# Windowed attention with a SoLU layer behind it: the lower words of the 64-bit weights in 32 bits, and their minimum by GpSimd

## Chip, core and metric

One core of a Trainium2 chip runs the whole program. The metric is the device time of one execution in microseconds (us); of several runs the median counts. The engines are named as in the profile: PE (TensorE), DVE (VectorE), ACT (ScalarE), POOL (GpSimd) and SP (SyncE, whose queue issues all the transfers).

## What is computed

Attention in a window of 64 positions for 8 batches of 8 heads (576 positions, 64 columns a head), then for all 4608 tokens a matmul of 512x1024, a SoLU (the value times its softmax), a layer norm and a matmul of 1024x512. The weights come in as 64-bit words, two 32-bit words to a weight, and the core turns them into float32.

```python
def _attn_ref(q, k, v):
    scores = scale * np.matmul(q, k.transpose(0, 1, 3, 2))
    mask = (rel >= 0) & (rel < window)
    scores = np.where(mask, scores, -1000000000.0)
    attn = np.exp(scores - np.max(scores, axis=-1, keepdims=True))
    attn = attn / (np.sum(attn, axis=-1, keepdims=True) + 1e-09)
    return np.matmul(attn, v)

def _moe_ref(x, w_in, w_out, g_ln):
    h = x @ w_in
    e = np.exp(h - np.max(h, axis=-1, keepdims=True))
    solu = h * (e / (np.sum(e, axis=-1, keepdims=True) + 1e-09))
    mu, var = np.mean(solu, axis=-1, keepdims=True), ...
    return ((solu - mu) / np.sqrt(var + 1e-06) * g_ln) @ w_out
```

## The kernel before

The tokens run in 36 tiles of 128. A tile t goes through these steps, each of which stands in the trace under the name of the buffer that it writes: scores on PE (pS), the maximum of a head on DVE (sS and nmx), its exponential on ACT (sS), the scaling by the reciprocal of the sum on POOL (sS), the transposes on PE (pS again), their copies on ACT or DVE (PT), attention times values on PE (pO), the copy for the next matmul (xH), the first matmul (pH), the norm (mst, e), the transposes of e, and the second matmul (pO). The first tiles multiply in plain float32: tiles 0 to 2 in the first matmul (line 575) and tiles 0 and 1 in the second (line 707). All others multiply in three passes, with weights and data split in a rounded high part and the rest (lines 586 and 719). In the early tiles the attention's transposes are done by PE; later ones go by DMA.

The weights come as 8 blocks of 128 x 1024, blocks 0 to 3 of w_in and blocks 4 to 7 of w_out; block 0 is worked on in two halves of 512 columns. A block lands in a raw buffer, of which there are four, so that blocks 4 to 7 must wait for blocks 0 to 3 to be done. It is converted in five steps (function `weight_block`):

- ACT takes the upper words as float32, scales them and drops the sign into the buffer w (line 346);
- ACT turns the lower words into a small integer and writes it as 16 bits into the lower half of the upper word (line 348);
- DVE masks the upper half of the upper word, as 16-bit numbers, so that the sign alone stays (line 351);
- DVE limits w from above (line 353);
- DVE shifts w left by three bits and joins it with that upper word (line 355).

All operations are recorded by a planner first. It puts them in an order for each engine by due times, which it gets from a cost written beside each operation, and by a table of corrections (HINTS). The engines then run in that order: an instruction that waits holds up all that stand behind it on its engine. The due times run back from PE, whose own sequence is nearly as recorded.

Of the kernel before, what the change touches and what calls it, by code (L numbers as in the profile page):

```python
# [9 lines left out]
F32 = mybir.dt.float32  # L10
F32R = mybir.dt.float32r
BF16 = mybir.dt.bfloat16
U16 = mybir.dt.uint16
U32 = mybir.dt.uint32
I32 = mybir.dt.int32
AF = mybir.ActivationFunctionType
ALU = mybir.AluOpType
# [3 lines left out]
WIN = 64  # L21
BIG = 3.0e38

EXP_LO = 2.0 ** -15
EXP_HI = 122879.9921875
EXP_SCALE = 2.0 ** -112
NEG = -8.0e9
# [6 lines left out]
COLD = 23000  # L34

HINTS = {
    ("ACT", "PT", 0, 0): 1000, ("ACT", "mst", 0, 0): 3750, ("ACT", "raw", "w", 0): 3350,
# [3 lines left out]
    ("ACT", "raw", "w", 5): -65650, ("ACT", "w", 0, 5): -5850, ("DVE", "PT", 0, 5): 11750,  # L41
    ("ACT", "H", 0, 6): 1200, ("ACT", "w", 0, 6): -2400, ("DVE", "mst", 0, 6): 700, ("DVE", "sS", 0, 7): -400,
# [4 lines left out]
}  # L47
BEHIND = 2

EARLY = 3  # L50

PLAIN_IN = 3
SHARED = (0, 1, 2, 3, 4, 5, 6, 7)
PLAIN_OUT = 2

CROSS_FROM = 3
# [165 lines left out]
def tile_window_attention_solu_moe(  # L222
# [17 lines left out]
    nc = tc.nc  # L240
# [5 lines left out]
    H = 2 * NPAIR  # L246
    D = P // 2
# [27 lines left out]
    for first in (0, None, 1):  # L275
        t = masks[first] = const.tile([P, P], F32, name=f"mask{first}")
# [11 lines left out]
    plan = Plan(RINGS, NTILE, NW)  # L288

    def T(tag, n, shape, dtype=F32, pool=None):  # L290

        if (tag, n) not in plan.tiles:
            plan.tiles[tag, n] = (pool or sb).tile(
                shape, dtype, tag=tag, name=f"{tag}_{n}", bufs=RINGS[tag])
        return plan.tiles[tag, n]
# [8 lines left out]
    def W32(i):  # L304
        return T("w", i, [P, 2, 512])
# [9 lines left out]
    def weight_block(i, src):  # L315

        def raw():
            return T("raw", i, [P, 2, 512, 2], I32)  # L320

        def t():
            return W32(i).bitcast(I32)

        def tf():
            return W32(i)

        def lo():
            return raw()[:, :, :, 0]

        def hi():
            return raw()[:, :, :, 1]

        def half(k):
            return raw().bitcast(U16).rearrange("p a n (w k) -> p a n w k", k=2)[:, :, :, 1, k]


        parts = (0, 1) if i == 0 else (slice(0, 2),)
        for x in parts:
            n = 1024 if i else 512  # L340
            R, W = ("raw", i, x), ("w", i) if i else ("w", i, x)
            plan.dma(P * 8 * n, lambda x=x: nc.sync.dma_start(
                raw()[:, x].rearrange("p a n w -> p a (n w)" if i else "p n w -> p (n w)"), src[:, x]), [], [R])
            if i in SHARED:
                A, B = R + ("sign",), R + ("low",)
                plan.op("ACT", n + 66, lambda x=x: nc.scalar.activation(  # L346
                    tf()[:, x], hi()[:, x].bitcast(F32), AF.Abs, scale=EXP_SCALE), [R], [W])
                plan.op("ACT", n + 66, lambda x=x: nc.scalar.activation(  # L348
                    half(0)[:, x], lo()[:, x].bitcast(U32), AF.Copy, bias=-0.47, scale=255 / 256 * 2.0 ** -29),
                    [R, W], [B])  # L350
                plan.op("DVE", n // 3 * 2 + (18 if i else 78), lambda x=x: nc.vector.tensor_scalar(
                    half(1)[:, x], half(1)[:, x], 0x8000, 0, ALU.bitwise_and, ALU.bitwise_or), [R, W], [A], port=True)
                plan.op("DVE", n // 3 * 2 + (18 if i else 78), lambda x=x: nc.vector.tensor_scalar_min(
                    tf()[:, x], tf()[:, x], EXP_HI * EXP_SCALE), [W], [W], port=True)
                plan.op("DVE", n + 170, lambda x=x: nc.vector.scalar_tensor_tensor(
                    t()[:, x], t()[:, x], 3, hi()[:, x], ALU.logical_shift_left, ALU.bitwise_or),
                    [R, A, B], [W], port=True)
                continue
            plan.op("ACT", n + 66, lambda x=x: nc.scalar.activation(
                tf()[:, x], hi()[:, x].bitcast(F32), AF.Abs), [R], [W])  # L360
            plan.op("DVE", n // 3 * 2 + (18 if i else 78), lambda x=x: nc.vector.tensor_scalar(
                tf()[:, x], tf()[:, x], EXP_LO, EXP_HI, ALU.max, ALU.min), [W], [W], port=True)
            plan.op("DVE", n // 3 * 2 + (18 if i else 78), lambda x=x: nc.vector.tensor_scalar(
                t()[:, x], t()[:, x], 0x07FFFFFF, 3, ALU.bitwise_and, ALU.logical_shift_left), [W], [W], port=True)
            plan.op("DVE", n + 170, lambda x=x: nc.vector.scalar_tensor_tensor(
                t()[:, x], hi()[:, x], -0x40000000, t()[:, x], ALU.bitwise_and, ALU.bitwise_or), [R, W], [W], port=True)
            plan.op("DVE", n + 170, lambda x=x: nc.vector.scalar_tensor_tensor(
                t()[:, x], lo()[:, x], 29, t()[:, x], ALU.logical_shift_right, ALU.bitwise_or), [R, W], [W], port=True)

    def prep(i):  # L370
        if i < NC:
            weight_block(i, w_in[i * P:(i + 1) * P, :].rearrange("p (a n) -> p a n", a=2))
        else:
            f = 2 * (i - NC)
            weight_block(i, w_out[f * P:(f + 2) * P, :].rearrange("(a p) n -> p a n", p=P))
# [498 lines left out]
```

## Time and profile before

| what | value |
|---|---|
| runs | 528.54, 526.91, 528.2 us; median 528.2 |
| profiled execution | 526.66 us, its span 524.9 us |
| granted clock of PE | 0.999 |
| busy in the span | PE 505.3 us, DVE 403.0, ACT 372.4, POOL 301.4 |
| chain that ended last | PE 90%, ACT 8%, DMA 1% |
| HBM read and written | 50.86 MB and 9.44 MB |

The span runs from the first to the last instruction of the profiled execution; 1.76 us of that execution's time lie around it. A busy time says how long an engine worked, not whether anything waited for it. The chain of waits is followed back from the last instruction, at each step to what released it; the table of waits says which instruction of an engine stood still, and for whom; the windows cut the span in stretches and say how busy each engine was in each.

### The profile page before, as it was taken

Reading aid. Unit: us, or ns where it says so; the run is one execution under the profiler, and the core shown is the slowest. Engines: PE = TensorE matmul, PEld = TensorE weight load, DVE = VectorE, ACT = ScalarE, POOL = GpSimd, SP = SyncE. Lnnn points to the kernel's source line nnn. Section 1 sums busy time; section 2 is a strip of 40 time slices with the busy share of each in tenths; the row PEclk is TensorE's granted clock in tenths of the full one; section 3 lists DMA queues with packets and bytes.
Section 4 is the critical chain, followed back from the end, with each engine's and each line's share of the span. In section 5 each row is a group of like instructions: output and inputs, shape, how many; then the busy total and the mean of one; then the engine's idle time right before and its main releaser. Section 6 shows DMA issues by size and latency. Waiting matters only on the chain.

```text
span 524.9 us, 11600 instructions
## 1 busy us (share of the span) xinstructions
PE 505.3 (96%) x4072; PEld 394.2 (75%) x4072; DVE 403.0 (77%) x1174; ACT 372.4 (71%) x968; POOL 301.4 (57%) x550
## 2 busy tenths in 40 slices
PE   2798999999999999999999999999999999999996
PEld 2445576788787878888888888888888878888775
DVE  4887988979796978787878787878788688877631
ACT  5999996868686767676686868676858486766331
POOL 2038287584858485848384848584848384746420
PEclk9999999999999999999999999999999999999999
DMA  8994226976788888787999796969796979554301
GB/s 328 404 402 149 92 47 137 250 161 147 158 227 160 205 168 223 157 220 154 226 149 235 131 251 131 253 136 246 145 239 126 217 156 216 114 128 104 77 21 41
DMA packets 148507, 93.57 MB, mean 178 GB/s; under 512 B 132960, under 2 KB 132960, under 8 KB 148064
## 3 DMA queue, kind: packets, MB, share of 16 engines
q1 hardware_dynamic: 148448, 92.83, 72.9%
q8 instruction: 32, 0.52, 0.4%
q14 instruction: 27, 0.22, 0.1%
HBM read 50.86 MB, written 9.44 MB: 115 GB/s over the span
## 4 chain that ended last, share of the span: by engine, by line
PE 90%; ACT 8%; DMA 1%; DVE 0%; issue 0%; SPq 0%; ACTq 0%
PE pO L719 36%; PE pH L586 35%; PE pO L543 7%; PE pS L446 6%; ACT raw L348 3%; PE pO L707 3%; ACT sS L466 2%; ACT w L346 1%; PE pH L575 1%; DMA raw<-w_in 1%; PE pS L683 1%; ACT PT L524 1%; ACT e L603 0%; PE pS L519 0%; ACT xH L553 0%; DVE yL L694 0%
## 5 line engine op out<-in xcount | busy, mean ns | idle before, releaser
L484 POOL TENSOR_SCALAR sS<-sS,rec 128x128 f32<-128x128 f32 x280 | 151.8, 561 | 50.1 <-DVE rec L482 40.8
L466 ACT ACTIVATE sS<-sS,nmx 128x128 f32<-128x128 f32 x288 | 111.4, 389 | 2.1 <-DVE nmx L461 2.1
L719 PE MATMUL pO<-w_outH,yH 128*128 128x512 f32 x272 | 110.2, 405 | 0.0
L719 PE MATMUL pO<-w,yH 128*128 128x512 f32 x272 | 108.0, 397 | 0.0
L719 PE MATMUL pO<-w_outH,yL 128*128 128x512 f32 x272 | 106.8, 393 | 0.0
L586 PE MATMUL pH<-w_inH,xH 128*128 128x512 f32 x264 | 105.9, 401 | 0.0
L586 PE MATMUL pH<-w,xH 128*128 128x512 f32 x264 | 104.2, 398 | 0.0
L586 PE MATMUL pH<-w_inH,xL 128*128 128x512 f32 x264 | 103.6, 392 | 0.0
L498 ACT COPY raw<-sS 128x1024 uint16<-128x1024 uint16 x62 | 64.9, 1047 | 28.3 <-POOL sS L484 28.3
L623 POOL TENSOR_SCALAR e<-e,mst 128x512 f32<-128x512 f32 x72 | 72.9, 1021 | 3.9
L508 DVE COPY PT<-raw 128x1024 uint16<-128x1024 uint16 x62 | 50.1, 808 | 32.4 <-DMA raw<-raw 32.3
L557 ACT CAST xH<-pO 128x512 fp32r<-128x512 f32 x33 | 19.3, 584 | 62.2 <-PE pO L543 62.2
L719 PEld LDWEIGHTS pO<-w_outH,yH 128*128 128x128 f32 x272 | 51.0, 187 | 14.9 <-issue 2.4
L719 PEld LDWEIGHTS pO<-w_outH,yL 128*128 128x128 f32 x272 | 51.1, 188 | 12.8
L601 DVE TENSOR_REDUCE mst<-pH 128x1 f32<-128x1024 f32 x36 | 44.0, 1221 | 21.4 <-PE pH L586 21.1
L586 PEld LDWEIGHTS pH<-w_inH,xH 128*128 128x128 f32 x264 | 49.5, 187 | 13.6 <-DVE mst L606 0.2
L719 PEld LDWEIGHTS pO<-w,yH 128*128 128x128 f32 x272 | 51.1, 188 | 10.9
L609 POOL TENSOR_SCALAR mst<-mst 128x1 f32<-128x1 f32 x36 | 18.1, 501 | 71.5 <-DVE mst L606 65.4
L586 PEld LDWEIGHTS pH<-w_inH,xL 128*128 128x128 f32 x264 | 49.6, 188 | 12.6 <-DVE xL L558 0.2
L586 PEld LDWEIGHTS pH<-w,xH 128*128 128x128 f32 x264 | 49.6, 188 | 11.5 <-issue 0.2
L612 ACT ACTIVATE sq<-e,mst 128x1024 bf16<-128x1024 f32 x36 | 41.4, 1150 | 20.5 <-POOL mst L609 20.5
L615 POOL TENSOR_SCALAR mst<-mst 128x1 f32<-128x1 f32 x36 | 13.7, 380 | 73.3 <-DVE mst L611 38.5
(66 smaller groups left out, 856.6 us busy)
## 6 DMA issues: line engine op xcount, KB each, us to landing
qk<-qk SPq DMA_DIRECT2D x36, 640.0 KB, 5.5
v<-vS SPq DMA_DIRECT2D x36, 512.0 KB, 5.5
y<-ot SPq DMA_DIRECT2D x36, 256.0 KB, 2.5
raw<-w_out SPq DMA_DIRECT2D x4, 1024.0 KB, 9.6
raw<-w_in SPq DMA_DIRECT2D x3, 1024.0 KB, 11.0
raw<-raw SPq DMA_TRANSPOSE x124, 3.2
raw<-w_in SPq DMA_DIRECT2D x2, 512.0 KB, 5.8
g_sb<-gT SPq DMA_DIRECT2D x1, 4.0 KB, 13.3
```

Source lines behind the costliest of these rows:

```text
L446: nc.tensor.matmul(PS(t)[half * WIN:(half + 1) * WIN, r, p], q[rs, p, half * WIN:(half + 1) * WIN], keys, start=True, stop=True)
L466: plan.op("ACT", 390, lambda h=h: nc.scalar.activation(SS(t)[:, h], SS(t)[:, h], AF.Exp, bias=cols("nmx", h), scale=-1.0, accum_out=cols(" ...
L484: plan.op(engine, cost, lambda h=h: v.tensor_scalar(SS(t)[:, h], SS(t)[:, h], rec()[:, h:h + 1], 0.0, ALU.mult, ALU.add), [R], [("sS", t, ...
L498: plan.op("ACT", 1050, lambda x=x: nc.scalar.copy(XP(t)[:, x], SS(t)[:, 4 * x:4 * x + 4].bitcast(U16).rearrange("p h (n w) -> p w (h n)", ...
L508: plan.op("DVE", 740, lambda x=x: nc.vector.tensor_copy(PT(t)[:, 4 * x:4 * x + 4].bitcast(U16).rearrange("p h (n w) -> p h w n", w=2), XP( ...
L543: nc.tensor.matmul(PX(t)[r * D:(r + 1) * D, p, ks], V(t, half)[:, h * D:(h + 1) * D], PT(t)[:, h, ks], start=True, stop=True)
L557: plan.op("ACT", 560, lambda: nc.scalar.copy(XH(t), PX(t)), [("pO", NTILE + t)], [("xH", t)])
L586: plan.op("PE", 235, lambda n=n, c=c, x=x, w=w: nc.tensor.matmul(PH(t)[:, hs], x(t)[:, c], WH(c, h) if w is WH else WL(c)[:, h], start=(n ...
L601: plan.op("DVE", 1225, lambda: nc.vector.tensor_reduce(nmax(), PH(t), axis=AX.X, op=ALU.max, negate=True), [("pH", t)], [key(0)])
L612: plan.op("ACT", 1150, lambda: nc.scalar.activation(T("sq", t, [P, DFF], BF16), E(t), AF.Square, bias=nmean(), scale=1.0, accum_out=ss()), ...
L623: plan.op("POOL", 770, lambda h=h, hs=hs: nc.gpsimd.tensor_scalar(E(t)[:, hs], E(t)[:, hs], nmean(), kk(), ALU.add, ALU.mult), [key(4), ke ...
L719: plan.op("PE", 235, lambda f=f, i=i, x=x, k=k, y=y, w=w: nc.tensor.matmul(PO(), y(t)[:, f], w(i, x), start=(f == k == 0), stop=(f == NF - ...
```

## The change

The lower words stay where they are. ACT converts them in place and writes them as 32-bit words (line 352 of the changed kernel) in place of the 16-bit write into the upper word. DVE's mask of the sign goes. Two DVE instructions of the shift-and-join kind take the place of one: the first joins the sign of the upper word with the converted lower word, the second shifts w and joins it with that (lines 376 and 379). The minimum goes from DVE to POOL, in halves of 512 columns (line 363). With these go new costs for the planner and a new table of corrections, which set the order on all engines; the sequence of the first 20 transfers on SP stays as it was, and PE's sequence changes in the first three tiles only.

```diff
 HINTS = {
...
-    ("ACT", "raw", "w", 5): -65650, ("ACT", "w", 0, 5): -5850, ("DVE", "PT", 0, 5): 11750,
...
+    ("DVE", "rec", 0, 4): -4300, ("DVE", "y", 0, 4): 82050, ("ACT", "raw", "w", 5): -119200,
...
-SHARED = (0, 1, 2, 3, 4, 5, 6, 7)
+HELPED = (0, 1, 2, 3, 4, 5, 6, 7)
+MASKED = 0
...
-            if i in SHARED:
-                A, B = R + ("sign",), R + ("low",)
-                plan.op("ACT", n + 66, lambda x=x: nc.scalar.activation(
-                    tf()[:, x], hi()[:, x].bitcast(F32), AF.Abs, scale=EXP_SCALE), [R], [W])
-                plan.op("ACT", n + 66, lambda x=x: nc.scalar.activation(
-                    half(0)[:, x], lo()[:, x].bitcast(U32), AF.Copy, bias=-0.47, scale=255 / 256 * 2.0 ** -29),
-                    [R, W], [B])
-                plan.op("DVE", n // 3 * 2 + (18 if i else 78), lambda x=x: nc.vector.tensor_scalar(
-                    half(1)[:, x], half(1)[:, x], 0x8000, 0, ALU.bitwise_and, ALU.bitwise_or), [R, W], [A], port=True)
-                plan.op("DVE", n // 3 * 2 + (18 if i else 78), lambda x=x: nc.vector.tensor_scalar_min(
-                    tf()[:, x], tf()[:, x], EXP_HI * EXP_SCALE), [W], [W], port=True)
-                plan.op("DVE", n + 170, lambda x=x: nc.vector.scalar_tensor_tensor(
-                    t()[:, x], t()[:, x], 3, hi()[:, x], ALU.logical_shift_left, ALU.bitwise_or),
-                    [R, A, B], [W], port=True)
-                continue
...
+            ab = 1139 if i else 644
+            plan.op("ACT", ab, lambda x=x: nc.scalar.activation(
+                tf()[:, x], hi()[:, x].bitcast(F32), AF.Abs, scale=EXP_SCALE), [R], [W])
+            if not MASKED:
+                plan.op("ACT", ab + (206 if i else 69), lambda x=x: nc.scalar.activation(
+                    lo()[:, x], lo()[:, x].bitcast(U32), AF.Copy, bias=-0.47, scale=255 / 256 * 2.0 ** -29), [R], [B])
+            halves = [x] if i == 0 else [0, 1]
...
+            if helped:
+                for y in halves:
+                    plan.op("POOL", 720, lambda y=y: nc.gpsimd.tensor_scalar_min(
+                        tf()[:, y], tf()[:, y], EXP_HI * EXP_SCALE), [W], [W + (y,)])
...
+                plan.op("DVE", n + 200, lambda x=x: nc.vector.scalar_tensor_tensor(
+                    lo()[:, x], hi()[:, x], -0x80000000, lo()[:, x], ALU.bitwise_and, ALU.bitwise_or),
+                    [R], [B], port=True)
+                plan.op("DVE", n + 200, lambda x=x: nc.vector.scalar_tensor_tensor(
+                    t()[:, x], t()[:, x], 3, lo()[:, x], ALU.logical_shift_left, ALU.bitwise_or),
+                    [R, B], [W, *C], port=True)
```

ACT, from the conversion of block 3 to the copies of the transposes of tile 1, before. Block 3 is raw_155 and w_265, block 4 is raw_250 and w_295; sS_247 and PT_343 belong to tile 1, sS_314 to tile 2.

```order
L346 ACTIVATE w_265<-raw_155 128x1024
L348 ACTIVATE raw_155<-raw_155 128x1024
L466 ACTIVATE sS_247,sm_253<-sS_247,nmx_248 128x128 x7
L346 ACTIVATE w_295<-raw_250 128x1024
L348 ACTIVATE raw_250<-raw_250 128x1024
L466 ACTIVATE sS_314,sm_321<-sS_314,nmx_315 128x128 x2
L524 COPY PT_343<-pS_324 128x512
L466 ACTIVATE sS_314,sm_321<-sS_314,nmx_315 128x128
L603 ACTIVATE e_360,mst_332<-pH_212,mst_332 128x1024
L553 COPY xH_377<-pO_350 128x256
L524 COPY PT_343<-pS_324 128x512
```

The same place in the changed kernel: block 3 is raw_154 and w_258, block 4 is raw_262 and w_303, block 5 is raw_267; sS_235 and PT_344 belong to tile 1, sS_321 to tile 2.

```order
L349 ACTIVATE w_258<-raw_154 128x1024
L352 ACTIVATE raw_154<-raw_154 128x1024
L479 ACTIVATE sS_235,sm_252<-sS_235,nmx_236 128x128 x7
L352 ACTIVATE raw_262<-raw_262 128x1024
L349 ACTIVATE w_303<-raw_262 128x1024
L352 ACTIVATE raw_267<-raw_267 128x1024
L537 COPY PT_344<-pS_327 128x512
L479 ACTIVATE sS_321,sm_346<-sS_321,nmx_322 128x128
L616 ACTIVATE e_362,mst_333<-pH_254,mst_333 128x1024
L566 COPY xH_381<-pO_349 128x256
L537 COPY PT_344<-pS_327 128x512
```

The lower words of block 5 now stand ahead of the first copy of tile 1's transposes, and two exponentials of tile 2 went behind it. Further up in the queue the same instructions stand in both, in an order that differs a little.

POOL, from its first instruction on a tile or a weight, before: sS_247, sS_314 and sS_399 are the scores of tiles 1, 2 and 3, the mst are small columns of the norm.

```order
L484 TENSOR_SCALAR sS_247<-sS_247,rec_289 128x128 x8
L609 TENSOR_SCALAR mst_332<-mst_332 128x1
L484 TENSOR_SCALAR sS_314<-sS_314,rec_429 128x128 x8
L484 TENSOR_SCALAR sS_399<-sS_399,rec_461 128x128 x8
L609 TENSOR_SCALAR mst_464<-mst_464 128x1
```

The same place in the changed kernel, where sS_235, sS_321 and sS_406 are the scores of tiles 1, 2 and 3, w_137, w_180, w_220 and w_258 are blocks 0 to 3, and w_303 and w_429 are blocks 4 and 5:

```order
L363 TENSOR_SCALAR w_137<-w_137 128x512 x2
L363 TENSOR_SCALAR w_180<-w_180 128x512 x2
L363 TENSOR_SCALAR w_220<-w_220 128x512 x2
L363 TENSOR_SCALAR w_258<-w_258 128x512 x2
L497 TENSOR_SCALAR sS_235<-sS_235,rec_291 128x128 x6
L363 TENSOR_SCALAR w_303<-w_303 128x512 x2
L497 TENSOR_SCALAR sS_235<-sS_235,rec_291 128x128 x2
L622 TENSOR_SCALAR mst_333<-mst_333 128x1
L363 TENSOR_SCALAR w_429<-w_429 128x512
L497 TENSOR_SCALAR sS_321<-sS_321,rec_434 128x128 x8
L363 TENSOR_SCALAR w_429<-w_429 128x512
L497 TENSOR_SCALAR sS_406<-sS_406,rec_460 128x128 x4
```

The minimum of block 4 now stands between the scaled heads of tile 1, and the two halves of block 5 stand ahead of tile 2 and of tile 3.

More of the change, by code (lines that the diff above doesn't have):

```diff
@@ L22 @@
 BIG = 3.0e38
-EXP_LO = 2.0 ** -15
 EXP_HI = 122879.9921875
@@ L36 @@
 HINTS = {
-    ("ACT", "PT", 0, 0): 1000, ("ACT", "mst", 0, 0): 3750, ("ACT", "raw", "w", 0): 3350,
[3 rows of a table removed]
-    ("ACT", "raw", "w", 5): -65650, ("ACT", "w", 0, 5): -5850, ("DVE", "PT", 0, 5): 11750,
-    ("ACT", "H", 0, 6): 1200, ("ACT", "w", 0, 6): -2400, ("DVE", "mst", 0, 6): 700, ("DVE", "sS", 0, 7): -400,
[4 rows of a table removed]
+    ("ACT", "mst", 0, 0): 3700, ("ACT", "raw", "w", 0): 34400, ("ACT", "xH", 0, 0): 3450,
+    ("DVE", "w", 0, 0): 1100, ("ACT", "mst", 0, 1): 6800, ("ACT", "w", 0, 1): -1800,
+    ("POOL", "sS", 0, 1): 26650, ("ACT", "mst", 0, 2): -22350, ("ACT", "xH", 0, 2): 800,
+    ("PE", "pS", 0, 2): -3200, ("ACT", "raw", "w", 3): 1150, ("ACT", "yH", 0, 3): 87000,
+    ("DVE", "PT", 0, 3): -3700, ("DVE", "raw", "w", 3): 11950, ("DVE", "xL", 0, 3): -14900,
+    ("DVE", "y", 0, 3): 10000, ("POOL", "sS", 0, 3): -950, ("ACT", "xH", 0, 4): -300,
+    ("ACT", "yH", 0, 4): -10100, ("DVE", "e", 0, 4): 6450, ("DVE", "mst", 0, 4): 24250,
+    ("DVE", "rec", 0, 4): -4300, ("DVE", "y", 0, 4): 82050, ("ACT", "raw", "w", 5): -119200,
+    ("ACT", "w", 0, 5): -8750, ("DVE", "e", 0, 5): 14000, ("ACT", "ot", 0, 6): 24300, ("ACT", "w", 0, 6): -4550,
+    ("DVE", "rec", 0, 6): -18500, ("DVE", "w", 0, 11): 17650, ("DVE", "w", 0, 13): 1300,
+    ("ACT", "sS", 0, 32): 52450, ("POOL", "sS", 0, 32): 28350, ("DVE", "mst", 0, 33): -10700,
[4 rows of a table added]
 }
@@ L332, in hi @@
             return raw()[:, :, :, 1]
-        def half(k):
-            return raw().bitcast(U16).rearrange("p a n (w k) -> p a n w k", k=2)[:, :, :, 1, k]
         parts = (0, 1) if i == 0 else (slice(0, 2),)
@@ L343, in weight_block @@
                 raw()[:, x].rearrange("p a n w -> p a (n w)" if i else "p n w -> p (n w)"), src[:, x]), [], [R])
-            if i in SHARED:
-                A, B = R + ("sign",), R + ("low",)
-                plan.op("ACT", n + 66, lambda x=x: nc.scalar.activation(
-                    tf()[:, x], hi()[:, x].bitcast(F32), AF.Abs, scale=EXP_SCALE), [R], [W])
-                plan.op("ACT", n + 66, lambda x=x: nc.scalar.activation(
-                    half(0)[:, x], lo()[:, x].bitcast(U32), AF.Copy, bias=-0.47, scale=255 / 256 * 2.0 ** -29),
-                    [R, W], [B])
-                plan.op("DVE", n // 3 * 2 + (18 if i else 78), lambda x=x: nc.vector.tensor_scalar(
-                    half(1)[:, x], half(1)[:, x], 0x8000, 0, ALU.bitwise_and, ALU.bitwise_or), [R, W], [A], port=True)
+            B = R + ("low",)
@@ new lines, in weight_block @@
+            S = R + ("sign",)
+            ab = 1139 if i else 644
[5 more added lines that the diff above has]
+            halves = [x] if i == 0 else [0, 1]
@@ new lines, in weight_block @@
+            helped = i in HELPED
+            C = [W + (y,) for y in halves] if helped else []
+            D = [S + (y,) for y in halves] if MASKED else []
+            for y in halves if MASKED else []:
+                plan.op("POOL", 770, lambda y=y: nc.gpsimd.tensor_scalar(
+                    hi()[:, y], hi()[:, y], -0x80000000, 0, ALU.bitwise_and, ALU.bitwise_or), [R, W], [S + (y,)])
+            if helped:
+                for y in halves:
+                    plan.op("POOL", 720, lambda y=y: nc.gpsimd.tensor_scalar_min(
+                        tf()[:, y], tf()[:, y], EXP_HI * EXP_SCALE), [W], [W + (y,)])
+            else:
@@ L353, in weight_block @@
                 plan.op("DVE", n // 3 * 2 + (18 if i else 78), lambda x=x: nc.vector.tensor_scalar_min(
                     tf()[:, x], tf()[:, x], EXP_HI * EXP_SCALE), [W], [W], port=True)
-                plan.op("DVE", n + 170, lambda x=x: nc.vector.scalar_tensor_tensor(
+            if MASKED:
+                plan.op("DVE", n + 200, lambda x=x: nc.vector.scalar_tensor_tensor(
                     t()[:, x], t()[:, x], 3, hi()[:, x], ALU.logical_shift_left, ALU.bitwise_or),
-                    [R, A, B], [W], port=True)
@@ L358, in weight_block @@
-                continue
[L359 to L368, printed above, removed]
+                    [R, *D], [W, *C], port=True)
+                plan.op("DVE", n + 200, lambda x=x: nc.vector.scalar_tensor_tensor(
+                    t()[:, x], lo()[:, x], 29, t()[:, x], ALU.logical_shift_right, ALU.bitwise_or),
+                    [R], [W], port=True)
+            else:
+                plan.op("DVE", n + 200, lambda x=x: nc.vector.scalar_tensor_tensor(
+                    lo()[:, x], hi()[:, x], -0x80000000, lo()[:, x], ALU.bitwise_and, ALU.bitwise_or),
+                    [R], [B], port=True)
+                plan.op("DVE", n + 200, lambda x=x: nc.vector.scalar_tensor_tensor(
+                    t()[:, x], t()[:, x], 3, lo()[:, x], ALU.logical_shift_left, ALU.bitwise_or),
+                    [R, B], [W, *C], port=True)
```

11 rows, old and new, of the table HINTS are left out of this document.

## The prediction

> **What bounds the kernel now.** I read the page's busy times first, then the windows, the table of PE's waits, and the chain of waits in the stretch where they lie.
>
> ```profile
> PE 505.3 (96%) x4072; PEld 394.2 (75%) x4072; DVE 403.0 (77%) x1174; ACT 372.4 (71%) x968; POOL 301.4 (57%) x550
> ```
>
> PE is busy for 505.3 of a span of 524.9 us. The windows show where the other 19.6 us lie; the columns are the stretch, its length, then the busy time (and count) of PE, weight loads, DVE, ACT and POOL, the granted clock, and the share and rate of the DMA engines.
>
> ```profile
> 20.00:30.00 10.00, 8.80 (x52) 4.21 (x44) 6.86 (x23) 9.24 (x22) 0.20 (x1) 1.00 1.02 402
> 30.00:40.00 10.00, 9.02 (x106) 5.26 (x99) 9.43 (x43) 9.94 (x26) 4.01 (x9) 1.00 1.01 396
> 40.00:50.00 10.00, 8.46 (x87) 5.10 (x87) 8.21 (x25) 9.78 (x27) 8.75 (x17) 1.00 0.38 122
> ...
> 100.00:500.00 400.00, 400.00 (x3279) 324.43 (x3279) 317.61 (x912) 279.24 (x752) 253.55 (x444) 1.00 0.79 175
> 500.00:524.90 24.90, 20.54 (x95) 15.87 (x93) 5.37 (x9) 6.55 (x11) 3.04 (x7) 0.98 0.09 33
> ```
>
> From 100 to 500 us PE is busy for 400.00 of 400 us: nothing that other engines do faster there can shorten it. At the end it idles for 4.4 us, but PE's sequence and the few operations of the last norm stand there as before. What the change can win lies in the first 60 us, where ACT is busy for 9.2 to 9.9 of every 10 us and the DMA engines are full until 40 us. PE's waits say the same, all of them before 50 us:
>
> ```profile
> PE pO L543 <- ACT PT L524: 2.9, 2, 1.7
> PE pH L575 <- ACT xH L553: 1.6, 1, 1.6
> PE pS L519 <- ACT PT L524: 1.0, 1, 1.0
> PE pS L519 <- POOL sS L484: 0.9, 2, 0.5
> ```
>
> So the front of the program is ACT's queue, and a microsecond that it wins there reaches the end as long as no other wait takes its place. The chain of waits (start, length, what) shows that queue:
>
> ```profile
> 7.21 1.54 ACT sS L466 x8
> ...
> 33.27 0.48 ACT PT L524
> 33.75 0.39 ACT sS L466 x2
> 34.14 1.09 ACT e L603 x2
> 35.24 0.32 ACT xH L553
> 35.56 0.49 ACT PT L524
> ...
> 38.23 1.06 ACT w L346
> ```
>
> An exponential with its accumulator read takes 1.54 / 4 = 0.385 us, and a conversion of upper words (line 346) 1.06 us from start to start.
>
> **The change, part by part.** The instructions of the conversion (shortest, median and longest in ns; of nine, seven are of 1024 columns and two of 512):
>
> ```profile
> L346 ACT ACTIVATE w<-raw x9: 644/1144/1227, 6.5 to 52.4; 128x1024 f32<-128x1024 f32 x7, 128x512 f32<-128x512 f32 x2
> L351 DVE TENSOR_SCALAR raw<-raw x9: 734/1311/1411, 7.5 to 54.8; 128x1024 uint16<-128x1024 uint16 x7, 128x512 uint16<-128x512 uint16 x2
> L348 ACT ACTIVATE raw<-raw x9: 1324/2514/2528, 10.8 to 54.0; 128x1024 uint16<-128x1024 uint32 x7, 128x512 uint16<-128x512 uint32 x2
> L355 DVE SCALAR_TENSOR_TENSOR w<-w,raw x9: 693/1225/1601, 12.1 to 56.7; 128x1024 int32<-128x1024 int32 x7, 128x512 int32<-128x512 int32 x2
> ...
> L353 DVE TENSOR_SCALAR w<-w x9: 420/726/894, 11.5 to 55.9; 128x1024 f32<-128x1024 f32 x7, 128x512 f32<-128x512 f32 x2
> ```
>
> DVE loses nine masks (2 x 0.73 + 7 x 1.31 = 10.6 us) and nine minima (2 x 0.42 + 7 x 0.73 = 5.9 us) and gets nine more joins (2 x 0.69 + 7 x 1.23 = 10.0 us): 6.5 us less. I cost that at nothing, since the chain in the front runs on ACT; if DVE did come to bound, the first join of a block is the place, as it now waits for ACT's lower words and holds DVE's queue.
>
> ACT's lower words cost 2 x 1.32 + 7 x 2.51 = 20.2 us now. No row shows the new form, an ACTIVATE that reads and writes 32-bit words at every second place. The nearest row is line 346, of the same engine, count and 32-bit type, with the same stride on the reading side, at 1.144 us. The other end is line 348's own 2.514 us, since the slow part may be the integer input and not the 16-bit output. I take 1.144 (1.06 from start to start) and keep 2.51 as a rival.
>
> The Trainium skill's page "ScalarE: Activation LUTs", section "What ACT_TABLE_LOAD costs", gives an ACTIVATE with immediate scale and bias 186 ns plus 0.833 ns an element, for every function, fp32 and bf16 alike; the estimate from that for 1024 columns is 1.04 us. Line 346 agrees within a tenth, while line 348 stands at 2.51 us, so a type or a place can cost what the rule doesn't have. By the rule the sum below would stay where it is, as a transfer ends last there.
>
> POOL gets 16 minima of 128x512. Its nearest row is line 623, of that shape; two windows (POOL's column is the fifth) show eight scalings of 128x128 with and without DVE at work in the same memory.
>
> ```profile
> L623 POOL TENSOR_SCALAR e<-e,mst x72: 757/1106/1692, 51.8 to 509.4; 128x512 f32<-128x512 f32 x72
> 40.00:45.20 5.20, 0.00 (x0) 5.10 (x8) 1.00 0.25 99
> 46.30:49.20 2.90, 0.00 (x0) 2.80 (x8) 1.00 0.73 226
> ```
>
> A minimum costs 0.76 us when undisturbed and at most 1.69; sixteen are 12 to 27 us, on an engine that is busy for 13 of the 30 us from 20 to 50. Eight scalings take 2.8 us while DVE reads PSUM and 5.1 us beside DVE's masks, minima and joins.
>
> **How the path moves.** The place to count is the first copy of tile 1's transposes on ACT (33.3 us in the chain). Ahead of it stand, before and now, the same conversions of upper words and the same copies; the lower words of blocks 0 to 4 become those of blocks 0 to 5, and 18 exponentials become 16. Without waits ACT would be there at 33.3 - 5 x 2.51 + 6 x 1.06 - 2 x 0.385 = 26.3 us, 7.0 us earlier. But two of these blocks have to land first:
>
> ```profile
> 17.38 0.39 SPq L342 DMA_DIRECT2D raw<-w_out  x1
> raw<-w_out SPq DMA_DIRECT2D x1, 1024.0 KB, 8.8
> 21.81 0.38 SPq L342 DMA_DIRECT2D raw<-w_out  x1
> raw<-w_out SPq DMA_DIRECT2D x1, 1024.0 KB, 6.9
> ```
>
> Block 4 lands at 17.38 + 8.8 = 26.2 us and block 5 at 21.81 + 6.9 = 28.7 us, in a stretch where the DMA engines are full (share 1.02 and 1.01) and the sequence of transfers is as before. An earlier issue moves these landings little; I take them as they are. After 26.2 us ACT still has block 4's lower and upper words and, from 28.7 us, block 5's lower words: the copy starts at 28.7 + 1.06 = 29.8 us. **Of the 7.0 us that ACT saves there, 3.5 are left; the rest becomes a wait for transfers.** If block 5 landed two microseconds sooner, block 4 would bound at 26.2 + 3 x 1.06 = 29.4 us, so this matters little.
>
> From that copy the next five operations of ACT are the same in both orders (copy, exponential, e, xH, copy), 0.48 + 0.39 + 1.09 + 0.32 + 0.49 us, so the first matmul of tile 1 moves by the same 3.5 us, if POOL keeps up. POOL scales six heads of tile 1, then waits for block 4's upper words (28.3 us), does its two minima (29.8) and scales the last two heads (30.5); they are needed at 29.8 + 0.5 + 0.4 + 1.1 + 0.3 = 32.1 us. That leaves 1.6 us.
>
> ```profile
> 36.72 7.13 PE L575 MATMUL pH<-w,xH 128*128 128x512 f32 x16
> 49.21 1.88 PE L575 MATMUL pH<-w,xH 128*128 128x512 f32 x4
> 51.37 5.32 PE L575 MATMUL pH<-w,xH 128*128 128x512 f32 x12
> 59.71 7.13 PE L707 MATMUL pO<-w,yH 128*128 128x512 f32 x16
> ```
>
> Tile 1's first matmul then runs from 33.2 to 40.3 us. Between it and tile 2's stands POOL. On ACT seven exponentials and xH follow the second copy, so block 5's upper words end at 32.1 + 0.5 + 2.7 + 0.3 + 1.1 = 36.7 us; the first half of its minimum ends at 37.5, tile 2's heads at 40.3 (2.8 us) or 42.6 (5.1), the other half at 41.1 or 43.4, tile 3's heads with a small column between at 44.3 or 48.9. ACT, with eight exponentials, two operations of 1.1 us, a copy and e in between, reaches tile 2's second copy at about 44 us. PE's transposes of tile 3 take 0.5 us, so tile 2's first matmul starts between 45 and 49.4 us and, at 7.1 us, ends between 52 and 56.5; now it ends at 56.6. That is a gain of 4.5 at best and nearly nothing at worst. I take the quick row for most of it, because in that stretch DVE's queue holds maxima and sums from PSUM and waits for the exponentials, with one pair of joins: 3.5 us.
>
> Behind it PE has no wait now, in the same sequence as before. The second matmul of tile 0 (59.71, then 56.2) needs block 7: its upper words on ACT by about 49 us, POOL's four minima of blocks 6 and 7 behind the two halves of e by 51 (54 at the slow price), a join of 1.23 us. That is done before 56.2 in both cases. The other queues keep their sequence from there but for a few rows, such as a store that SP now issues ahead of two loads; with 400.00 of 400 us busy on PE and DVE at 318 I cost those at nothing, as DVE's free fifth hides them.
>
> The sum against the profiled execution's own 526.66 us: 526.66 - 3.5 = 523.2 us. The median of the runs shown, 528.2, stands 1.5 us higher, so the forecast there is **524.7 us**. A difference of 0.3% (1.6 us) is about what a measurement of this kernel can tell from none.
>
> **The rivals.** First, that POOL takes the place of ACT. The heads of tiles 2 and 3 stand behind block 5's minima, and beside DVE's two joins each block a scaling costs 0.64 in place of 0.35 us. Then tile 2's first matmul starts at 48.5 to 49.4 us, and 0.1 to 1 us is left: 526.66 - 0.6 = 526.1, at the median 527.6 us. For it speaks the slow window above; against it that in the new order DVE mostly waits there. I give it 0.16. The Trainium skill states a rule on this, on the page "SBUF — State Buffer", section "SBUF: two separate sides": GpSimd and VectorE share a port pair that is locked for a whole instruction by a GpSimd operation or by a VectorE operation with two inputs in that memory, and the loser waits it out. The two windows agree with that rule, and by it the move of the minimum to GpSimd beside more joins is wrong.
>
> Second, on the slower side, that the lower words get no cheaper, because the integer input and not the 16-bit output is what costs 2.51 us. Then ACT has six of them ahead of tile 1's copy and not five, and two exponentials fewer: 2.51 - 0.77 = 1.7 us later at the point that sets the front, and no transfer hides it. The time would be 526.66 + 1.7 = 528.4, at the median 529.9 us. It decides from 6 x = 5 x 2.51 + 0.77, that is x = 2.2 us an instruction. For it speaks that no row has a 32-bit integer input without the slow price; against it that 16-bit output at every fourth place is just as much unlike all the quick rows. This is also the case in which the change doesn't do what it says. I give it 0.12.
>
> **How the numbers follow.** The forecast has 0.72. Its own range goes from a gain of 4.7 us at the profiled execution's level (522.0) to one of 1.8 us at the median's (526.4). The first rival at 527.6 is taken in, so the range ends at 528.2; the second, with 0.12, is left out above. Faster by over 0.3% is the forecast alone, 0.72; within 0.3% the first rival, 0.16; slower the second, 0.12.
>
> **What would show it.** The lower words' row should read 1.1 to 1.4 us; 2.2 or more makes the forecast wrong. ACT's queue should show a new wait, for a transfer from w_out, of some 2 us before block 4. Tile 1's first matmul should start near 33.2, tile 2's end near 53, tile 0's second start near 56.2 us, and from 100 to 500 us PE should be busy throughout. Scalings of tiles 2 and 3 at 0.6 us each, with PE waiting for POOL, would be the first rival.

## The result and the profile after

The changed kernel takes 533.04 us (median of 533.47, 533.36, 532.71 and 531.99), the kernel before, on the same chip, 528.04 us: a ratio of 1.0099 with a 95% interval of 1.0081 to 1.0118. It is slower by 1%; the forecast was 0.7% faster. The profiled execution of the changed kernel has a span of 531.7 us, 6.8 us more than before's 524.9, and a granted clock of 0.988 in place of 0.999. (The medians differ by 5.0 us; what follows accounts for the 6.8 of the two profiled executions.)

The page after, busy times and the chain that ended last, by engine and by line:

```profile
PE 507.5 (95%) x4072; PEld 395.9 (74%) x4072; DVE 400.7 (75%) x1165; ACT 364.0 (68%) x968; POOL 331.7 (62%) x566
...
PE 87%; POOL 6%; DMA 2%; DVE 2%; ACT 1%; issue 1%; SPq 0%; ACTq 0%; DVEq 0%
PE pO L732 36%; PE pH L599 35%; PE pO L556 6%; PE pS L459 6%; PE pO L720 3%; POOL w L363 3%; POOL sS L497 2%; DMA raw<-w_in 2%; PE pS L696 1%; POOL e L636 1%; DVE w L379 1%; DVE raw L376 1%; ACT w L349 0%; PE pS L532 0%; DVE sS L474 0%
```

ACT had 8% of the chain before and has 1% now; POOL had none to speak of and has 6%. The two new instructions, by their lines (shortest, median and longest in ns):

```profile
L363 POOL TENSOR_SCALAR w<-w x16: 1483/1517/2567, 7.1 to 61.5; 128x512 f32<-128x512 f32 x16
...
L352 ACT ACTIVATE raw<-raw x9: 639/1155/1200, 11.2 to 53.8; 128x1024 int32<-128x1024 uint32 x7, 128x512 int32<-128x512 uint32 x2
```

The lower words fell from 2.51 to 1.155 us. The minimum costs POOL 1.52 us for 512 columns, twice the 0.76 us of the row that the prediction took, and never less than 1.48. PE's waits after, below the 5.0 us for the first transfer (total, times, longest, in us):

```profile
PE pS L532 <- ACT PT L537: 3.9, 1, 3.9
PE pS L532 <- DVE sS L497: 3.1, 1, 3.1
PE pS L532 <- POOL sS L497: 2.6, 1, 2.6
PE pO L720 <- DVE yH L701: 2.5, 1, 2.5
```

The first two of these rows end by 15.3 us, in tile 0; before, PE waited 3.3 us for the same heads on DVE and 1.7 us for a copy there. The last two are new, and both hang on POOL, as the chain of waits after shows (start, length, what; pieces under 0.1 us are left out):

```profile
13.85 3.57 POOL w L363 x2
...
26.02 1.23 DVE w L379
...
27.67 3.20 POOL sS L497 x6
30.87 2.91 POOL w L363 x2
33.78 1.45 POOL sS L497
35.28 0.83 PE pS L532 x2
36.11 1.92 PE pS L459 x32
38.02 1.07 PE pO L556 x16
...
41.03 1.04 ACT w L349
42.15 1.50 POOL w L363
43.65 2.81 POOL sS L497 x8
46.46 1.45 POOL w L363
47.92 2.47 POOL sS L497 x4
...
53.41 3.57 POOL e L636 x2
57.07 5.97 POOL w L363 x4
63.10 1.11 issue
64.21 0.69 DVE yH L701
64.94 8.83 PE pO L720 x16
```

From 42 to 63 us POOL is the chain almost without a gap. The four minima of blocks 6 and 7 end at 63.04. DVE's queue at that place (in brackets the idle time and what ended it):

```profile
60.07 1.62 DVE L379 SCALAR_TENSOR_TENSOR w<-w,raw 128x1024 int32<-128x1024 int32 x1 [3.71 <-POOL w L363]
...
63.06 1.23 DVE L379 SCALAR_TENSOR_TENSOR w<-w,raw 128x1024 int32<-128x1024 int32 x1 [0.36 <-POOL w L363]
64.21 1.28 DVE L701 TENSOR_TENSOR yH<-pS,g_sb 128x512 f32<-128x512 f32 x2
```

The second joins of blocks 6 and 7 wait there for the minima, and yH, for which PE waits, stands behind them. The three float32 matmuls after, on PE:

```profile
39.00 8.37 PE L588 MATMUL pH<-w,xH 128*128 128x512 f32 x16
52.38 7.03 PE L588 MATMUL pH<-w,xH 128*128 128x512 f32 x16
64.94 8.83 PE L720 MATMUL pO<-w,yH 128*128 128x512 f32 x16 [2.54 <-DVE yH L701]
```

Tile 1's first matmul starts 2.3 us later than before (39.00 against 36.72), tile 0's second 5.2 us later (64.94 against 59.71). Two of the three also take longer, 8.37 and 8.83 us where the same sixteen matmuls took 7.13. The windows tell why (the granted clock is the number behind POOL's count):

```profile
35.00:40.00 5.00, 4.72 (x51) 3.38 (x52) 3.08 (x21) 2.62 (x11) 0.82 (x3) 0.50 0.82 296
60.00:65.00 5.00, 2.46 (x68) 1.98 (x66) 4.57 (x5) 2.63 (x13) 4.30 (x4) 1.00 0.44 146
65.00:70.00 5.00, 5.00 (x8) 2.16 (x9) 4.93 (x10) 3.35 (x8) 0.21 (x1) 0.66 0.22 90
100.00:500.00 400.00, 400.00 (x3293) 324.50 (x3286) 322.79 (x944) 281.73 (x763) 254.05 (x442) 1.00 0.80 179
```

Behind PE's waits of 2.58 us (up to 35.28) and 2.54 us (up to 64.94) the clock is granted at 0.50 and 0.66 in these windows. Tile 0's second matmul starts 5.2 us late and takes 1.70 us longer: 6.9 us in all, the 6.8 us of the span. The 1.24 us of tile 1's first matmul don't come on top: the chain doesn't run through it, but from PE's scores (36.11) and attention (38.02) over ACT to POOL's minimum at 42.15. Those short steps of PE ran at 0.50 too: the transposes, scores and attention from 35.28 on took 0.83, 1.99 and 1.12 us, where the same steps take 0.44 (at 32.26), 1.10 (at 61.30) and 0.69 us (at 50.84) with the clock at 1.00. An estimate from these figures gives the clock 0.4 + 0.9 + 0.4 + 1.7 = 3.4 us and the waits proper the other 3.5; that nothing else would have held up ACT and POOL in between is not shown. (In the first 20 us the clock's column says less than it seems to: it reads 1.00 there, yet the same 32 scores take 1.98 us at 5.03 and 1.99 us at 17.42.) From 100 to 500 us PE is busy throughout, as before.

### The profile page after: what moved, and what is told of

It is laid out like the page before. It is cut to its first block, busy times and chain, and to the rows that moved or that the text cites. A ratio compares the mean times of both kernels' runs of the same rounds, so it can differ in the third digit from the quotient of the medians.

```text
span 531.7 us, 11605 instructions
## 1 busy us (share of the span) xinstructions
PE 507.5 (95%) x4072; PEld 395.9 (74%) x4072; DVE 400.7 (75%) x1165; ACT 364.0 (68%) x968; POOL 331.7 (62%) x566
## 4 chain that ended last, share of the span: by engine, by line
PE 87%; POOL 6%; DMA 2%; DVE 2%; ACT 1%; issue 1%; SPq 0%; ACTq 0%; DVEq 0%
PE pO L732 36%; PE pH L599 35%; PE pO L556 6%; PE pS L459 6%; PE pO L720 3%; POOL w L363 3%; POOL sS L497 2%; DMA raw<-w_in 2%; PE pS L696 1%; POOL e L636 1%; DVE w L379 1%; DVE raw L376 1%; ACT w L349 0%; PE pS L532 0%; DVE sS L474 0%
## 5 line engine op out<-in xcount | busy, mean ns | idle before, releaser
L636 POOL TENSOR_SCALAR e<-e,mst 128x512 f32<-128x512 f32 x72 | 74.1, 1038 | 3.8
L599 PEld LDWEIGHTS pH<-w_inH,xH 128*128 128x128 f32 x264 | 49.5, 187 | 13.5 <-ACT sS L479 0.2
L479 ACT ACTIVATION_READ_ACCUMULATOR sS<-sS,nmx 128x1 f32 x288 | 54.2, 188 | 0.0
```

Of the source, the lines that this page charges most:

```text
L479: plan.op("ACT", 390, lambda h=h: nc.scalar.activation(SS(t)[:, h], SS(t)[:, h], AF.Exp, bias=cols("nmx", h), scale=-1.0, accum_out=cols(" ...
L599: plan.op("PE", 235, lambda n=n, c=c, x=x, w=w: nc.tensor.matmul(PH(t)[:, hs], x(t)[:, c], WH(c, h) if w is WH else WL(c)[:, h], start=(n ...
L636: plan.op("POOL", 770, lambda h=h, hs=hs: nc.gpsimd.tensor_scalar(E(t)[:, hs], E(t)[:, hs], nmean(), kk(), ALU.add, ALU.mult), [key(4), ke ...
```

## The experiments

All times below are medians; ratios are to runs of the kernel before on the same chip, with 95% intervals.

| kernel | time, us | ratio |
|---|---|---|
| e1, minimum with two operations | 523.69 | 0.9934 (0.9909 to 0.9959) |
| e12, the same again | 523.20 | 0.9922 (0.9909 to 0.9934) |
| e2, multiplication and addition | 523.15 | 0.9917 (0.9903 to 0.9932) |
| e7, one multiplication | 532.79 | 1.0102 (1.0086 to 1.0119) |
| e9, quick minimum twice | 532.55 | 1.0104 (1.0084 to 1.0124) |
| e10, quick minimum three times | 543.69 | 1.0312 (1.0291 to 1.0333) |
| e3, minimum on DVE, new table | 525.30 | 0.9967 (0.9953 to 0.9981) |
| e4, minimum on DVE, old table | 525.00 | 0.9961 (0.9947 to 0.9974) |
| e13, e4 again | 526.14 | 0.9973 (0.9959 to 0.9987) |
| e5, planner told 1500 | 533.44 | 1.0110 (1.0065 to 1.0154) |
| e11, quick minimum, planner told 610 | 524.46 | 0.9946 (0.9933 to 0.9959) |
| e14, quick minimum, whole blocks | 526.62 | 0.9982 (0.9974 to 0.9991) |

**The form of POOL's instruction.** The first theory was that a minimum as such is dear on POOL (T1); its rivals were the form with one operation (T2), VectorE in the same memory (T3) and the new order of work (T4). Three kernels keep the order of the changed kernel and edit line 363 alone.

```diff
-    nc.gpsimd.tensor_scalar_min(tf()[:, y], tf()[:, y], EXP_HI * EXP_SCALE)
+    nc.gpsimd.tensor_scalar(tf()[:, y], tf()[:, y], EXP_HI * EXP_SCALE, 0.0, ALU.min, ALU.max)  # e1
+    nc.gpsimd.tensor_scalar(tf()[:, y], tf()[:, y], 1.0, 0.0, ALU.mult, ALU.add)  # e2
+    nc.gpsimd.tensor_scalar_mul(tf()[:, y], tf()[:, y], 1.0)  # e7
```

> The minimum on GpSimd is written as a tensor_scalar with two operations (minimum, then maximum with 0), in the same order of work. T1, the operation minimum itself costs GpSimd about 1.5 us per 128x512 whatever the form: line 363 stays at 1.4 to 1.6 us, the time at 533 +- 1. T2, the form with one operation is the slow one, and the minimum isn't: line 363 falls to 0.76 to 0.95 us and the time to 525 to 527.

> The sixteen GpSimd instructions of line 363 keep their places and shape and become a multiplication by 1 and an addition of 0, the form of the scalings (this leaves out the upper limit of the weights). T1, only the price of the minimum makes the loss: line 363 falls to 0.76 to 0.95 us, tile 1's first matmul starts near 36 and tile 0's second near 58 us or earlier, the time falls to 524 to 527, below before's 528. T3, GpSimd is slow there because VectorE works in the same memory: line 363 stays above 1.2 us and the time near 533. T4, the new order of work is at fault whatever the price: line 363 falls to 0.8 us, and the time stays at 531 to 533.

> Line 363 becomes a multiplication by 1 in the form with one operation, in the same order (the upper limit of the weights is left out). T2a, the form with one operation is what costs GpSimd 1.5 us, whatever the operation: line 363 stays at 1.4 to 1.6 us, the time at 532 to 534. T2b, a minimum alone is dear and only a second operation beside it makes it cheap: line 363 at 0.6 us as in the run with two operations, the time at 523 to 524.5.

Line 363 in e1, the minimum with two operations:

```profile
L363 POOL TENSOR_SCALAR w<-w x16: 608/612/1596, 7.8 to 52.2; 128x512 f32<-128x512 f32 x16
```

In e2, the multiplication with the addition:

```profile
L363 POOL TENSOR_SCALAR w<-w x16: 612/619/1581, 7.3 to 51.8; 128x512 f32<-128x512 f32 x16
```

In e7, the multiplication alone:

```profile
L363 POOL TENSOR_SCALAR w<-w x16: 1481/1514/2047, 7.4 to 60.8; 128x512 f32<-128x512 f32 x16
```

The three rows and the row of the changed kernel make a square: one operation costs 1.52 us as a minimum and 1.51 as a multiplication, two cost 0.61 and 0.62. So T1 falls, though I held it: the minimum isn't dear, the form with one operation is, and the second operation, which changes no value here (the weights' absolute values are never below 0), makes it 2.5 times as fast. T2 holds, and both row and time came out better than it had expected (0.61 in place of 0.76 to 0.95, 523.7 in place of 525 to 527; e2's 523.15 also lies below its range of 524 to 527). T4 falls with the same runs, since the order is that of the changed kernel and the time is some 9 us less. Of T3 this much is right: the longest of these instructions take 1.58 to 2.57 us in every form, and the mean in e1 is 0.86 us, so something, and VectorE's work in the same memory is the candidate, does hold some of them up. It doesn't make the loss.

The Trainium skill, on the page "GPSIMD Engine Reference", section "3.1 Elementwise — side-by-side cycle accounting", says that a body with k up to 2 is bound by its read and write ports at 1.03 cycles an element. With k read as the operations an element, one operation and two would cost the same by that. The rows differ by 2.5, the wrong way round; for this instruction the measurement decides.

The float32 matmuls of e1, to be held beside those of the changed kernel:

```profile
34.32 7.13 PE L588 MATMUL pH<-w,xH 128*128 128x512 f32 x16 [0.45 <-DVE mst L619]
46.45 7.03 PE L588 MATMUL pH<-w,xH 128*128 128x512 f32 x16
56.41 7.13 PE L720 MATMUL pO<-w,yH 128*128 128x512 f32 x16
```

Tile 0's second matmul starts 8.5 us earlier than in the changed kernel and 3.3 us earlier than before, none takes longer than 7.13, and the clock of the run is 1.000.

**A dose of POOL time.** If POOL's time alone makes the loss, quick instructions that add up to as much must make it too.

```diff
-    nc.gpsimd.tensor_scalar(..., ALU.min, ALU.max)
+    [nc.gpsimd.tensor_scalar(..., ALU.min, ALU.max) for _ in range(2)][-1]  # e10: range(3)
```

> The minimum in the quick form (0.61 us) is issued twice in a row in each of the sixteen places, in the same order; the result is the same. If the time that GpSimd spends there is all that made the loss, 1.22 us a place in place of 0.61 or 1.5 gives a time between the two: 527 to 531. If the slow instruction did harm in another way too (by holding the memory's port against VectorE), two quick ones cost much less than that: 524 to 526.

> The same, three times in a row: 1.83 us a place. By GpSimd's time alone: above the changed kernel, 534 to 539, with TensorE waiting for GpSimd's heads and minima before 65 us and the granted clock below 0.9 in some stretch of 30 to 75 us. If the slow instruction did harm in another way: below 531.

POOL's groups by line (the first two numbers behind the bar are the total in us and the mean in ns); first e1:

```profile
L363 POOL TENSOR_SCALAR w<-w 128x512 f32<-128x512 f32 x16 | 13.5, 856 | 14.7 <-ACT w L349 14.6
```

The changed kernel:

```profile
L363 POOL TENSOR_SCALAR w<-w 128x512 f32<-128x512 f32 x16 | 25.8, 1625 | 12.6 <-ACT w L349 12.5
```

The quick form twice (e9):

```profile
L363 POOL TENSOR_SCALAR w<-w 128x512 f32<-128x512 f32 x32 | 26.3, 828 | 14.3 <-ACT w L349 12.9
```

Three times (e10):

```profile
L363 POOL TENSOR_SCALAR w<-w 128x512 f32<-128x512 f32 x48 | 35.9, 754 | 12.9 <-ACT w L349 10.2
```

The time follows the total: 13.5 us of it give 523.7, 25.8 give 533.0, 26.3 give 532.6, and 35.9 give 543.7 us. I had expected less of e9 (527 to 531), because I counted 2 x 0.61 us a place; with the mean of 0.83 its total equals that of the changed kernel, and so does the time, to half a microsecond. So the slow form needs no other harm to explain the loss than the time that it holds POOL. From e1 to the changed kernel a microsecond on POOL costs 9.35 / 12.3 = 0.76 us (0.71 by the ratios, as the two were measured at different times), and from e9 to e10 11.1 / 9.6 = 1.2 us: the waits grow, and in e10 the clock of the run is 0.983. e10 lies above its range of 534 to 539; that the price of a microsecond rises was not foreseen.

**The planner's price.** The planner counts 720 for the slow instruction.

```diff
-    plan.op("POOL", 720, lambda y=y: nc.gpsimd.tensor_scalar_min(
+    plan.op("POOL", 1500, lambda y=y: nc.gpsimd.tensor_scalar_min(
```

> The changed kernel as it is, with the slow minimum, but the planner is told 1500 instead of 720 for it and orders the work anew. If only a wrong cost in the planner put GpSimd on the path, it recovers a part: 527 to 531. If sixteen times 1.5 us don't fit into GpSimd's queue in the front in any order that this planner finds, it stays at 531 to 534. The table of hints was made for the other order, which may cost something by itself.

533.44 us: by the median nothing is won back, though the four runs lie far apart (530.0 to 535.4). The order did change, and with it the waits of PE, in e5 now, without those for the first transfer and in tile 0:

```profile
PE pH L588 <- DVE mst L619: 2.6, 1, 2.6
...
PE pS L532 <- POOL sS L497: 0.5, 1, 0.5
```

The wait for POOL's heads is down from 2.6 to 0.5 us, and one of 2.6 us for the norm's column on DVE is there in its place, behind which sixteen matmuls take 8.83 us. From 20 to 72 us the chain of waits holds no instruction of POOL any more; it goes over DVE and PE. So to get POOL off the path was not enough in this order. That no order would do is not shown: the table of corrections was made for another sequence.

**The minimum back on DVE.** This is the first half of the change alone, e3 with the new table, e4 and e13 with the old one.

```diff
-HELPED = (0, 1, 2, 3, 4, 5, 6, 7)
+HELPED = ()
```

> The minimum goes back to VectorE for all blocks, the 32-bit lower words stay, and so does the new table of hints (the planner orders the work anew). T1: GpSimd is out of the path, ScalarE keeps its gain, and the time is below before's: 524 to 527. T4, the new table is what loses: 530 or more. A table that was made for another sequence may also cost a microsecond or two by itself, in which case the run with the old table tells more.

> The minimum goes back to VectorE, the 32-bit lower words stay, and the table of hints is the one of before: this is the first half of the change alone. T1: lower words at 1.15 us, tile 1's copy on ScalarE at 29 to 31 us (before 33.2), no wait of TensorE for GpSimd of over 1 us, the time 524 to 527. If it stays at 528 or above, ScalarE's gain is lost to something other than GpSimd's minimum (transfers, VectorE), and T1 is wrong in its second half.

> The minimum on VectorE with the 32-bit lower words and the old table once more, more rounds: 524.5 to 526 us, 0.3 to 0.5% below before. The part of the gain that belongs to the lower words alone.

The gain is there, 0.3 to 0.4% in the three runs, and the last one misses its range by 0.1 us. But not the way that I had expected: the copy of tile 1's transposes on ACT comes at 32.27 us in e4 and not at 29 to 31, and tile 1's first matmul hardly moves (36.72 before):

```profile
36.40 7.11 PE L583 MATMUL pH<-w,xH 128*128 128x512 f32 x16 [0.19 <-DVE mst L618]
```

It waits for the norm's columns on DVE. The chain of waits of e4 just ahead of it:

```profile
35.11 1.14 DVE e L614
...
36.25 0.08 DVE mst L618
```

Ahead of these the chain has eight maxima on DVE, from 33.33 us on. With ACT quicker, DVE ends last at this place. That this is what keeps the gain small is not shown: DVE ends last there in e3 and e12 too, where the matmul starts at 34.49 and 34.13 us, and e3's time is no better than e4's. In e13's profile, taken of a run of 527.20 us, it starts at 37.94.

**Best version, the halves, the price of 610.** The quick form again, beside the kernel with the minimum on DVE; then one instruction of 1024 columns a block, and the planner told the measured price.

```diff
-            halves = [x] if i == 0 else [0, 1]
+            halves = [x]  # e14, at a planner's cost of 1440
-                    plan.op("POOL", 720, ...
+                    plan.op("POOL", 610, ...  # e11
```

> The minimum on GpSimd in the form with two operations once more, more rounds: 523 to 525 us, 0.5 to 0.9% below before. If moving the minimum to GpSimd is worth something by itself, it is also at least 0.2% below the kernel that keeps the minimum on VectorE, measured beside it.

> The quick form on GpSimd, but a whole block of 1024 columns in one instruction and not two halves of 512 (the planner is told 1440, the sum of the halves, and may order a few rows anew). If the price goes by columns, an instruction takes 1.15 to 1.25 us undisturbed and the time is within 1.5 us of the halves, 523 to 526. If the halves matter, because heads and other small work on GpSimd wait behind a long instruction: 526 to 529.

> The quick form on GpSimd, and the planner is told 610 instead of 720 for it, as measured; it orders some rows anew. With the cost 0.11 us nearer to the truth in 16 places I expect nothing that can be measured beside the halves with 720: 522.5 to 525. If the table of hints fits only the order that it was made for, 525 or more.

e12 and e2 (523.20 and 523.15 us) are the fastest, and of the two only e12 limits the weights. e12 is 4.1 us below before, and by the ratios 1.8% below the changed kernel, so it beats both. It is 0.5% below e13, measured beside it, and their intervals don't meet: with the quick form the whole change is worth more than the lower words alone. (Order and table differ between the two, so how much of the half per cent is DVE's relief isn't told apart.) e14 is 3.4 us slower than e12, within the range of the theory that the halves matter, though the instruction itself came out cheaper than expected (median 1.04 us, 1.15 to 1.25 expected). PE's waits for POOL and for the norm's columns in e14:

```profile
PE pS L532 <- POOL sS L497: 1.5, 2, 0.8
PE pH L588 <- DVE mst L619: 1.2, 2, 0.6
```

In e1 and e12 PE didn't wait for POOL's heads at all. But the long instruction doesn't explain these 1.5 us: in e14 one of 1.03 us stands among tile 1's heads, in e12 two halves of 1.19 us together. What differs is that the heads start at 29.45 us in e14, behind reciprocals on DVE, and at 26.84 in e12. PE also waits 1.8 us for joins on DVE (line 379), which it doesn't in e12. The planner has ordered the work anew in e14, so that the halves are worth anything by themselves is not shown. e11 stands 1.3 us above e12 with intervals that meet at one end: a truer price in the planner brought nothing.

## Why the prediction was wrong

**What bounds the kernel.** Right: all that was lost, and in e12 all that was won, lies before 75 us, with PE at 400.00 of 400 us from 100 to 500 us. The prediction's table of PE's waits begins below its two longest rows, 4.5 us for the first transfer and 3.3 us for DVE's heads; both lie before 10 us and are still there after, so the reading stands.

**ACT's lower words.** Right: 1.155 us against 1.144 taken. The second rival (2.51, 529.9 us) didn't come; that the time ended on its side has another cause.

**The price of POOL's minimum.** This is the step that failed. "A minimum costs 0.76 us when undisturbed and at most 1.69" was taken from a row of the same engine, shape and operation name (TENSOR_SCALAR), line 623. But that instruction has two operations and the new one has one, which the profile's row doesn't show and the source does. Undisturbed it costs 1.48 us, and with two operations 0.61 (e1): the form, not the minimum, was mispriced. The upper bound of 27 us for all sixteen did hold (25.8 us), and my mistake was to lead the path with the lower one: I tried the dear price on the heads and on blocks 6 and 7, but not on the minima that stand ahead of tiles 1 to 3.

**The slack of 1.6 us.** POOL's heads of tile 1 start at 27.67, the two minima behind the first six take 2.91 us in place of 1.5 and end at 33.78, not 29.8, the last two heads take 1.45 in place of 0.7, and PE's last transposes of tile 1 come at 35.28. The copy that needed them at 32.1 comes at 36.14. The six heads, which were to be done before 28.3, start late for the same cause one step ahead, but for a part only: they wait for reciprocals on DVE that stand behind a join (26.02 in the chain), and DVE's second joins wait for POOL's minima (13.85). With the quick form (e12) they start at 26.84, 0.8 us earlier, and end at 29.9, so the forecast had them too early whatever the price of the minimum, and nearly all the slack was gone there too: the last two heads end at 31.8.

**ACT's seven microseconds, of which 3.5 are left.** Right in kind: the copy comes at 31.02 (29.8 forecast, 33.18 before), behind a wait of 1.49 us for block 4, whose work starts at 27.50 and not at 26.2. ACT, in the changed kernel from the first of these blocks to the second copy:

```profile
27.50 1.15 ACT L352 ACTIVATE raw<-raw 128x1024 int32<-128x1024 uint32 x1 [1.49 <-DMA raw<-w_out]
...
29.97 1.17 ACT L352 ACTIVATE raw<-raw 128x1024 int32<-128x1024 uint32 x1 [0.24 <-DMA raw<-w_out]
31.02 0.56 ACT L537 COPY PT<-pS 128x512 f32<-128x512 f32 x1
...
36.14 0.59 ACT L537 COPY PT<-pS 128x512 f32<-128x512 f32 x1 [2.73 <-PE pS L532]
```

The 2.2 us that ACT has won at 31.02 become a wait of 2.73 us at 36.14, for transposes that wait for POOL.

**Tile 2's matmul and tile 0's second one.** 52.38 in place of 45 to 49.4 us, and 64.94 in place of 56.2; the four minima of blocks 6 and 7, put at 51 or 54, end at 63.04. With the quick form (e1) the same steps give 46.45 and 56.41 us, and the time is 523.2 to 523.7 against 524.7 forecast: the rest of the sum was right to a microsecond or so.

**DVE's lighter load at nothing.** As a load it was nothing; what the sum left out is that DVE's queue now stands behind POOL's minima. The second joins wait 6.5 us for them in four places, and the reciprocals of tile 1 and yH stand behind such joins. It was also too simple in general: with ACT quick and the minimum left on DVE, DVE ended last at tile 1's first matmul in e4, and the gain was 0.3 to 0.4% where e12 has 0.8%. DVE ends last at that matmul in e12 too, so that its load makes this difference is argued and not shown.

**The first rival.** Its place was right, POOL instead of ACT. Its price was not: the eight scalings of tile 2 take 2.81 us, the quick 0.35 each. And I let it end at no gain, where a queue that has become the chain can also lose; a clock that falls behind a wait was no term of the sum, and by the estimate above it made 3.4 of the 6.8 us.

The Trainium skill's page "TensorE: Matmul & The Clock Gate", section "Part 1: The HAM clock gate (the "warmup" mystery)", gives two states of the clock, full and half, and half after an idle window of about 3.4 us. The window with 0.50 agrees on the half; on the idle time the trace differs, as waits of 2.58 and 2.54 us, with some shorter ones around the first, were already enough.

## What to carry to other kernels

Before an instruction is moved to another engine, find a row of the same engine with the same form, the number of its operations included, and where there is none, walk the whole path once with the dear end of the range. On GpSimd try an elementwise operation with a constant as a tensor_scalar with two operations, the second of which changes nothing; here that was shown for a minimum and a multiplication of 128x512 float32 in place. Where an engine gets work that stands ahead of a transfer of heads or weights to TensorE, price the wait twice: once for itself, and once for the clock behind it.

## What I had not expected of the hardware

- GpSimd's tensor_scalar on 128x512 float32 takes 1.48 to 1.52 us undisturbed with one operation (minimum or multiplication) and 0.61 with two.
- POOL's queue, on the path of this kernel, passed on nearly all that it got: 0.7 to 1.2 us of the kernel's time for each microsecond.
- The granted clock stood at 0.50 for five microseconds behind a wait of 2.58 us in the middle of a busy program, and sixteen matmuls took 8.4 us in place of 7.1; behind a wait of 2.54 us another sixteen took 8.8.
